# Decoding the last chunk of two token matrices in the mix stage instead of in attention

## The chip, the cores and the metric

The kernel runs on one core of a Trainium2 chip. The metric is device time in microseconds (us) of one execution. Engines by the names of the profile: PE is TensorE (matmuls; PEld its weight loads), DVE is VectorE, ACT is ScalarE, POOL is GpSimd, SP is SyncE, which here only issues transfers. Each engine takes its instructions strictly in the order in which they stand.

## What is computed

Block-sparse attention (4 batches, 8 heads, 768 positions, 64 features a head, blocks of 32) and then a token and channel mix on its output.

```python
mask = |blk_i - blk_j| <= 1, or first or last block row or column, or 3 sampled blocks per row
attn = softmax(where(mask, q @ k.T / 8, -1e9));  x = (attn @ v), heads side by side   # (4, 768, 512)
theta = x @ w_theta
zr, zi = x * cos(theta), x * sin(theta)
y = einsum('ts,bsd->btd', w_tok_r, zr) + einsum('ts,bsd->btd', w_tok_i, zi)
u = x + y
out = u + maximum(u @ w_ch, 0)
```

The four weight matrices arrive as 64-bit numbers and are turned into pairs of 32-bit numbers, a high and a low part, on the chip: the "decoding" of this text. Every matrix product of the mix is done three times, high by high, high by low and low by high.

## The kernel before

**Attention.** A work list of 52 units: per pair of batches four wide units (first and last block rows) and 22 ordinary ones, one block row each. The order of all engines is written out by hand in a loop over the units (`manual_schedule`). For a unit, POOL gathers keys and values, PE makes the scores (L308), DVE the negated maximum (L310), ACT the exponentials (L319), PE turns them (L325), ACT copies them out (L327), PE weighs the values (L359), and after every second unit DVE normalises (L340 to L344) and SP writes the rows to a buffer `xs` in DRAM.

**Decoding.** A `Piece` is a stretch of columns of one weight matrix on 128 partitions. Its work is in three phases: `bits` (L71 to L73 on DVE, after L67 on ACT), `rest` (L79, L81) and `low` (L90, L91, after the cast L87 on ACT, which is `high`). The `Decoder` goes through a list of pieces; `ahead(n)` puts the ACT instructions of the next n phases into the order and `go(n)` the DVE ones. Two pieces' raw words are loaded at first, and a piece's load (L62) is issued on SP when the piece two places before it has had its last phase. In attention the list holds `w_theta` (4 pieces of 512 columns) and both token matrices (9 each): 22 pieces, 66 phases, spread over the units by weight (no phases in the first and last two units).

A token matrix is six chunks of 128 rows by 768 columns. Chunks 0 and 1 have tiles of their own (`w_tok_r_hi`, ...). Chunks 2 to 5 go to a `room` that attention uses for keys or values at first, and that is taken over (`settle`) when the first piece for it is cast.

**The mix.** 48 steps, 12 a batch: step k has batch b, half h of the channels (6 steps each) and chunk j of the tokens. For a step PE makes the angles (`theta`, L654 to L656), ACT and DVE reduce them (`reduced`, L661 to L666), ACT takes sine and cosine, DVE multiplies by x (L681), ACT casts the high parts zh (L686) and DVE makes the low parts zl (L690), two steps before PE uses them in `mix` (24 matmuls, L706 to L708). For h = 0 DVE also turns rows (L637) and splits them (L646). SP loads x for a later step in eight transfers (L609, L622). After chunk 5 of a half DVE adds x (L719 to L722). A batch's eight output products (`out`, 12 matmuls, L729 to L731, into one bank, emptied by L734 and L735) wait in a list and are done two at a time in the second to fifth steps of the next batch, the last batch's at the end.

The first steps' preparation is woven into the last units of attention by hand. Steps 0 to 4 are also in the order written (`theta(k+2)`, `waves(k+1)`, `turn(k+3)`, `turned(k+1)`, `split(k+3)`, `reduced(k+2)`, loads, decoding, `mix(k)`); from step 5 on a scheduler, which simulates the engines, sets the order of each engine, and may draw an instruction of a later step into an earlier place. `w_ch` is decoded in the mix: 8 pieces of 256 columns, with `PHASES` (1, 1, 1, 3, 3) in steps 0 to 4 and 3 phases in each of steps 7 to 11.

Of the kernel before, what the change touches and what calls it, by code (L numbers as in the profile page):

```python
# [26 lines left out]
Q_BUFS = 3  # L27
XO_BUFS = 2
FIXED = 5
PHASES = (1, 1, 1, 3, 3)  # L30

# [551 lines left out]
def token_mix(tc, w, ch_pieces, xs, outT, bias, nb, fore):  # L585
# [7 lines left out]
    nc = tc.nc  # L593
    with ExitStack() as late, ExitStack() as ctx:
        half_pi, up_int, down_int, early = bias
# [3 lines left out]
        def at(k):  # L599
            return k // 12, (k // 6) % 2, k % 6  # L600
# [26 lines left out]
        def turn(k, tag="r"):  # L627
            b, h, j = at(k)
            if h:
                return  # L630
            if j % 3 == 0:
                tp = tps[min((2 * b + j // 3) % 3, 1)]
                xT[b, j // 3] = [tp.tile([P, 4, 384], F32R, tag=f"xT{x}", name=f"xT{x}{b}_{j}") for x in "hl"]
            raw = xr.pop((b, j))
            turning[k] = r = xp.tile([P, 4, 128], F32, tag=tag, name=f"r{k}", bufs=3 if tag == "xa" else 1)
            for c in range(4):
                nc.vector.transpose(r[:, c, :].rearrange("p (i t) -> p i t", t=32), raw[:, :, c])  # L637
# [10 lines left out]
        def theta(k):  # L648
            b, h, j = at(k)
            hi, lo = tok(b, j)  # L650
            wh, wl = [x[:, :, 256 * h : 256 * h + 256] for x in w["theta"]]
            angles[k] = ps = ps_h.tile([P, 512], F32, tag="h", name=f"h{k}")[:, 0:256]
            for c in range(4):
                nc.tensor.matmul(ps, hi[:, c, :], wh[:, c, :], start=c == 0, stop=False)  # L654
                nc.tensor.matmul(ps, hi[:, c, :], wl[:, c, :], start=False, stop=False)  # L655
                nc.tensor.matmul(ps, lo[:, c, :], wh[:, c, :], start=False, stop=c == 3)  # L656
# [11 lines left out]
        def waves(k):  # L668
            r = angles[k]
            cs = tz.tile([P, 256], F32, tag="cs", name=f"cs{k}")  # L670
            nc.scalar.activation(cs, r, AF.Abs)  # L671
            nc.scalar.activation(cs, cs, AF.Sin, bias=half_pi, scale=-1.0)
            nc.scalar.activation(r, r, AF.Sin)
            angles[k] = cs, r
# [17 lines left out]
        def turned(k):  # L692
            multiplied(k)
            highs(k)
            lows(k)
# [43 lines left out]
        place = vp.tile([P, 6, 260], F32, tag="vw", name="xr_first").rearrange("p c f -> p (c f)")  # L739
# [5 lines left out]
        decoder = Decoder(ch_pieces(), None, nc.sync, fore)  # L745
# [40 lines left out]
        for k in range(FIXED):  # L786
            theta(k + 2)
            waves(k + 1)
            turn(k + 3)
            turned(k + 1)  # L790
            split(k + 3)
            reduced(k + 2)
            load(k + 3)
            load_raw(k + 5)
            phases = PHASES[k] if k < len(PHASES) else 0
            decoder.ahead(phases)
            decoder.go(phases)
            mix(k)
# [4 lines left out]
        for k in range(FIXED, steps):  # L803
            b, h, j = at(k)
            if k + 4 < steps:
                load(k + 4)
            if k + 5 < steps:
                load_raw(k + 5)
            if k + 2 < steps:
                theta(k + 2)  # L810
                reduced(k + 2)
                waves(k + 2)
                turned(k + 2)
            if k + 3 < steps:
                turn(k + 3)
                split(k + 3)
            if k > 6 and decoder.left():
                decoder.ahead(3)
                decoder.go(3)
            mix(k)  # L820
            if h == 0 and b > 0 and 0 < j < 5:
                for _ in range(2):
                    out(*pending.pop(0), ps_o, "o")
            if h == 1 and j == 5:
                pending += [(b, th, e) for th in range(2) for e in range(4)]
# [4 lines left out]
def sparse_attention_then_token_mix(ctx, tc, qT, qE, kT, vr, sampled, w_theta, w_tok_r, w_tok_i, w_ch, outT):  # L830
    nc = tc.nc
    n_batch = outT.shape[0]
    const = ctx.enter_context(tc.tile_pool(name="const", bufs=1))
    ident = const.tile([P, P], F32, name="ident")
    make_identity(nc, ident)
    bias = []
    for name, value in (("half_pi", math.pi / 2), ("up_int", ROUND), ("down_int", -ROUND), ("early", 0.0)):
        bias.append(const.tile([P, 1], F32, name=name))
        nc.vector.memset(bias[-1], value)
    dram = ctx.enter_context(tc.tile_pool(name="dram", bufs=1, space=bass.MemoryType.DRAM))  # L840
    xs = [dram.tile([NB, 2, 32, 2, 2, P], F32, name=f"xs{bp}") for bp in range(NP)]

    w = {}
    w["theta"] = [const.tile([P, 4, 512], F32R, name=f"w_theta_{x}") for x in ("hi", "lo")]
    for name in ("tok_r", "tok_i"):
        w[name] = [const.tile([P, 2, 768], F32R, name=f"w_{name}_{x}") for x in ("hi", "lo")]

    def room(name, use, dtype=F32):
        return const.tile([P, 8, 768], dtype, tag=f"room_{name}", name=f"{use}_{name}")

    def settle(name):
        t = room(name, "w", F32R)
        w[name] = [x[:, j] for x in w[name] for j in range(2)]
        w[name] = [w[name][2 * x : 2 * x + 2] + [t[:, 4 * x + j] for j in range(4)] for x in range(2)]
        return [t[:, 4 * x : 4 * x + 4] for x in range(2)]

    words = {n: a.bitcast(I32) for n, a in dict(theta=w_theta, tok_r=w_tok_r, tok_i=w_tok_i, ch=w_ch).items()}

    def pieces(name, f, place, at=0, total=3072):
        if place:  # L860
            total = place[0].shape[1] * place[0].shape[2]
        made = []
        for f0 in range(0, total, f):
            made.append(Piece(nc, place, slice(f0, f0 + f), words[name][:, 2 * (at + f0) : 2 * (at + f0 + f)], f"{name}_{at + f0}"))
        return made


    fore = ctx.enter_context(tc.tile_pool(name="fore", bufs=2))
    follow = token_mix(tc, w, lambda: pieces("ch", 256, w["ch"], total=2048), xs, outT, bias, n_batch, fore)
    next(follow)  # L870
    early = pieces("theta", 512, w["theta"])
    early += [x for pair in zip(pieces("tok_r", 512, w["tok_r"]), pieces("tok_i", 512, w["tok_i"])) for x in pair]
    for name in ("tok_r", "tok_i"):
        place = []
        early += pieces(name, 512, place, 1536)
        early[-6].before = lambda name=name, place=place: place.extend(settle(name))
    attention(tc, qT, qE, kT, vr, sampled.bitcast(I32), xs, ident, early, room, follow)
    for _ in follow:
        pass
# [48 lines left out]
```

## Time and profile before

| | us |
|---|---|
| median of 3 runs (588.4 to 591.17) | 588.78 |
| the profiled execution | 592.62 |
| its span in the trace | 590.8 |
| first matmul of the mix, after the span's start | 252.9 |

The page gives the busy time of each engine, then the span in 40 slices of 14.77 us (a digit is the busy share in tenths). Matmuls overlap each other, so a busy PE is not PE at its peak. The chain of waits follows the work that ended last back to the start. In a group's row stand line, engine, operation, output and inputs, count, then busy us, mean ns of one, and the engine's idle time just before them with what ended it. A bracket in a timeline row is the idle time before that instruction and its releaser. A row of the table of stretches gives busy us and count of each engine that has work in it.

### The profile page before, as it was taken

Reading aid. Unit: us, or ns where it says so; the run is one execution under the profiler, and the core shown is the slowest. Engines: PE = TensorE matmul, PEld = TensorE weight load, DVE = VectorE, ACT = ScalarE, POOL = GpSimd, SP = SyncE. Lnnn points to the kernel's source line nnn. Section 1 sums busy time; section 2 is a strip of 40 time slices with the busy share of each in tenths; the row PEclk is TensorE's granted clock in tenths of the full one; section 3 lists DMA queues with packets and bytes.
Section 4 is the critical chain, followed back from the end, with each engine's and each line's share of the span. In section 5 each row is a group of like instructions: output and inputs, shape, how many; then the busy total and the mean of one; then the engine's idle time right before and its main releaser. Section 6 shows DMA issues by size and latency. Waiting matters only on the chain.

```text
span 590.8 us, 16785 instructions
## 1 busy us (share of the span) xinstructions
PE 538.4 (91%) x6636; PEld 475.3 (80%) x6636; DVE 442.8 (75%) x997; ACT 342.7 (58%) x730; POOL 148.6 (25%) x262
## 2 busy tenths in 40 slices
PE   4897878888977977999999999999999999999997
PEld 2564555656645645799999999999999999999996
DVE  3788788878897988888989976648857549547554
ACT  2677666868776876865657443456634547434510
POOL 1477758841775977000000000000000000000000
PEclk9999998999998989999999999999999999999999
DMA  8979999886698998644332341211432111212002
GB/s 293 340 223 344 308 332 348 287 267 223 185 299 257 304 307 225 193 121 131 108 85 76 96 130 59 72 45 54 130 92 70 50 53 42 80 56 75 2 1 107
DMA packets 63263, 95.60 MB, mean 162 GB/s; under 512 B 9168, under 2 KB 44624, under 8 KB 63184
## 3 DMA queue, kind: packets, MB, share of 16 engines
q1 hardware_dynamic: 56848, 71.09, 39.0%
q0 software_dynamic: 6336, 23.43, 12.2%
q8 instruction: 52, 0.85, 0.6%
q14 instruction: 27, 0.22, 0.1%
HBM read 81.90 MB, written 12.58 MB: 160 GB/s over the span
## 4 chain that ended last, share of the span: by engine, by line
PE 68%; DVE 15%; ACT 8%; issue 4%; DMA 4%; SPq 1%; ACTq 0%; DVEq 0%
PE y L706 11%; PE y L707 11%; PE y L708 11%; PE X L359 4%; PE o L730 4%; PE o L729 4%; PE o L731 4%; PE T L325 4%; DVE m L310 3%; PE h L655 3%; PE h L654 3%; PE h L656 3%; ACT P L319 3%; PE S L308 3%; PE SW L401 2%
## 5 line engine op out<-in xcount | busy, mean ns | idle before, releaser
L319 ACT ACTIVATE P<-S,m 128x256 f32<-128x256 f32 x176 | 69.5, 487 | 15.2 <-DVE m L310 15.2
L325 PE MATMUL T<-ident,P 128*128 128x128 f32 x352 | 50.9, 285 | 15.0 <-ACT pT L327 10.4
L310 DVE TENSOR_REDUCE m<-S 128x4 f32<-128x1024 f32 x44 | 53.6, 1217 | 12.3 <-PE S L308 12.3
L327 ACT COPY pT<-T 128x1024 f32<-128x1024 f32 x44 | 44.9, 1021 | 30.5 <-PE T L325 30.4
L325 PEld LDWEIGHTS T<-ident,P 128*128 128x128 f32 x352 | 38.8, 143 | 27.8 <-ACT pT L327 18.3
L291 POOL DMA_INDIRECT vb<-in_vr_dram,rows x44 | 46.3, 1052 | 48.8 <-PE X L359 43.3
L308 PE MATMUL S<-kg,q 64*32 64x256 f32 x1408 | 52.8, 394 | 5.9 <-issue 5.9
L661 ACT ACTIVATE t<-h,up_int 128x256 f32<-128x256 f32 x48 | 22.6, 474 | 59.7 <-PE h L656 56.0
L269 POOL COPY kg<-kb 128x256 f32 (+2 forms) x101 | 50.9, 544 | 15.8 <-PE S L308 15.8
L269 POOL COPY kg<-kb_tok_i 128x256 f32 (+2 forms) x101 | 49.4, 530 | 21.1 <-DMA kb_tok_i<-in_kT_dram 14.9
L654 PE MATMUL h<-w_theta_hi,xTh 128*128 128x256 f32 x192 | 54.1, 282 | 0.4 <-ACT xTh L645 0.4
L656 PE MATMUL h<-w_theta_hi,xTl 128*128 128x256 f32 x192 | 54.1, 282 | 0.2 <-DVE xTl L646 0.2
L655 PE MATMUL h<-w_theta_lo,xTh 128*128 128x256 f32 x192 | 53.9, 281 | 0.0
L706 PE MATMUL y<-w_tok_r,zh 128*128 128x384 f32 x128 | 43.1, 337 | 1.1 <-ACT zh L686 1.1
L706 PE MATMUL y<-w_tok_i,zh 128*128 128x384 f32 x128 | 43.1, 337 | 0.0
L707 PE MATMUL y<-w_tok_r,zh 128*128 128x384 f32 x128 | 43.1, 337 | 0.0
L707 PE MATMUL y<-w_tok_i,zh 128*128 128x384 f32 x128 | 43.1, 336 | 0.0
L708 PE MATMUL y<-w_tok_r,zl 128*128 128x384 f32 x128 | 43.0, 336 | 0.0
L730 PE MATMUL o<-ul,w_ch_hi 128*128 128x384 f32 x128 | 42.9, 335 | 0.0
L731 PE MATMUL o<-uh,w_ch_lo 128*128 128x384 f32 x128 | 42.9, 335 | 0.0
L729 PE MATMUL o<-uh,w_ch_hi 128*128 128x384 f32 x128 | 42.6, 336 | 0.1
L671 ACT ACTIVATE cs<-rr 128x256 f32<-128x256 f32 x48 | 19.7, 414 | 39.1 <-DVE rr L666 38.9
(155 smaller groups left out, 1427.4 us busy)
## 6 DMA issues: line engine op xcount, KB each, us to landing
xa<-xs SPq DMA_DIRECT2D x192, 64.0 KB
out_dram<-of SPq DMA_DIRECT2D x32, 192.0 KB
va<-in_vr_dram SPq DMA_DIRECT2D x22, 260.0 KB
q<-in_qT_dram SPq DMA_DIRECT2D x22, 256.0 KB
xs<-xo SPq DMA_DIRECT2D x88, 64.0 KB
xr<-xs SPq DMA_DIRECT2D x84, 64.0 KB
raw_tok_r<-in_w_tok_r_dram SPq DMA_DIRECT2D x9, 512.0 KB
raw_tok_i<-in_w_tok_i_dram SPq DMA_DIRECT2D x9, 512.0 KB
```

What stands on the lines that cost most here:

```text
L269: nc.gpsimd.tensor_copy(dst, blocks.rearrange("r g s f -> r s g f"))
L308: nc.tensor.matmul(sc[32 * p : 32 * p + 32, e, b, :], q[rows, b, p, :], keys[rows, :, :, place(b, p), :], start=True, stop=True)
L310: nc.vector.tensor_reduce(m, sc, axis=AX.X, op=ALU.min)
L319: nc.scalar.activation(pt[:, e, b, :], sc[:, e, b, :], AF.Exp, bias=m[:, e, b : b + 1], scale=-1.0)
L325: nc.tensor.transpose(t[:, k, :], pt, ident)
L654: nc.tensor.matmul(ps, hi[:, c, :], wh[:, c, :], start=c == 0, stop=False)
L655: nc.tensor.matmul(ps, hi[:, c, :], wl[:, c, :], start=False, stop=False)
L656: nc.tensor.matmul(ps, lo[:, c, :], wh[:, c, :], start=False, stop=c == 3)
L706: nc.tensor.matmul(acc, zh[:, dd], wh[j][:, tt], start=j == 0 and m == 0, stop=False)
L707: nc.tensor.matmul(acc, zh[:, dd], wl[j][:, tt], start=False, stop=False)
L708: nc.tensor.matmul(acc, zl[:, dd], wh[j][:, tt], start=False, stop=j == 5 and m == 1)
L730: nc.tensor.matmul(ps, wh[:, c, :], ul, start=False, stop=False)
```

## The change

Of the chunks 2 to 5 in the `room` of each token matrix, attention decodes the first 2304 of 3072 columns (chunks 2 to 4: four pieces of 512 and one of 256), so its list has 20 pieces and 60 phases. Chunk 5 of both, 768 columns each, is decoded in the mix by the decoder that decodes `w_ch`: six pieces of 256 columns ahead of the eight of `w_ch`. `PHASES` now covers steps 0 to 13: 18 phases in steps 0 to 4, which finish the six token pieces, 18 in steps 6 to 10 and 6 in steps 12 and 13, which are the eight pieces of `w_ch`. Mix step 5 is the first to need chunk 5. The output products of a batch go into the third, fourth and fifth step of the next batch, three, three and two; the second step has none. `w_ch` is complete with step 13, the second of batch 1. Line numbers above 30 grow by one.

```diff
-PHASES = (1, 1, 1, 3, 3)
+PHASES = (3, 3, 4, 4, 4, 0, 4, 4, 4, 3, 3, 0, 3, 3)
+LATER = 2304
@@ for k in range(FIXED): @@
-            phases = PHASES[k] if k < len(PHASES) else 0
+            phases = PHASES[k]
             decoder.ahead(phases)
             decoder.go(phases)
             mix(k)
@@ for k in range(FIXED, steps): @@
-            if k > 6 and decoder.left():
-                decoder.ahead(3)
-                decoder.go(3)
+            if k < len(PHASES):
+                decoder.ahead(PHASES[k])
+                decoder.go(PHASES[k])
             mix(k)
-            if h == 0 and b > 0 and 0 < j < 5:
-                for _ in range(2):
+            if h == 0 and b > 0:
+                for _ in range((0, 0, 3, 3, 2, 0)[j]):
                     out(*pending.pop(0), ps_o, "o")
@@ pieces @@
-    def pieces(name, f, place, at=0, total=3072):
-        if place:
-            total = place[0].shape[1] * place[0].shape[2]
+    def pieces(name, f, place, at=0, span=None):
         made = []
-        for f0 in range(0, total, f):
-            made.append(Piece(nc, place, slice(f0, f0 + f), words[name][:, 2 * (at + f0) : 2 * (at + f0 + f)], f"{name}_{at + f0}"))
+        first, last = span or (0, place[0].shape[1] * place[0].shape[2])
+        for f0 in range(first, last, f):
+            f1 = min(f0 + f, last)
+            made.append(Piece(nc, place, slice(f0, f1), words[name][:, 2 * (at + f0) : 2 * (at + f1)], f"{name}_{at + f0}"))
         return made
-    follow = token_mix(tc, w, lambda: pieces("ch", 256, w["ch"], total=2048), xs, outT, bias, n_batch, fore)
+    rests = dict(tok_r=[], tok_i=[])
+
+    def mix_pieces():
+        made = [x for n, place in rests.items() for x in pieces(n, 256, place, 1536, (LATER, 3072))]
+        return made + pieces("ch", 256, w["ch"], span=(0, 2048))
+
+    follow = token_mix(tc, w, mix_pieces, xs, outT, bias, n_batch, fore)
-    for name in ("tok_r", "tok_i"):
-        place = []
-        early += pieces(name, 512, place, 1536)
-        early[-6].before = lambda name=name, place=place: place.extend(settle(name))
+    for name, place in rests.items():
+        made = pieces(name, 512, place, 1536, (0, LATER))
+        made[0].before = lambda name=name, place=place: place.extend(settle(name))
+        early += made
```

## The prediction

> **What bounds the kernel now.** I read the page first: the busy line, the slices and the chain of waits.
>
> ```profile
> span 590.8 us, 16785 instructions
> PE 538.4 (91%) x6636; PEld 475.3 (80%) x6636; DVE 442.8 (75%) x997; ACT 342.7 (58%) x730; POOL 148.6 (25%) x262
> PE   4897878888977977999999999999999999999997
> DVE  3788788878897988888989976648857549547554
> DMA  8979999886698998644332341211432111212002
> PE 68%; DVE 15%; ACT 8%; issue 4%; DMA 4%; SPq 1%; ACTq 0%; DVEq 0%
> ```
>
> There are two stages. Up to about 252 us (slice 17, 14.77 us each) attention runs with nothing at nine tenths for long but the DMA engines. From slice 17 on TensorE is at nine tenths in every slice. The table of stretches then gives the room beside it (columns: stretch, length, busy us and count of PE, PEld, DVE, ACT, POOL, then granted clock, DMA share and GB/s).
>
> ```profile
> 28.00:125.00 97.00, 80.36 (x1940) 55.71 (x1938) 82.46 (x130) 71.50 (x142) 69.21 (x115) 0.98 0.93 298
> 147.00:244.00 97.00, 80.17 (x1936) 56.57 (x1935) 83.32 (x132) 71.27 (x143) 65.61 (x109) 0.96 0.87 260
> 257.00:285.00 28.00, 28.00 (x186) 28.00 (x185) 23.77 (x76) 17.71 (x44) 0.00 (x0) 1.00 0.47 134
> 285.00:324.00 39.00, 37.73 (x239) 37.20 (x238) 36.32 (x109) 25.16 (x68) 0.00 (x0) 1.00 0.29 81
> 371.00:400.00 29.00, 29.00 (x185) 29.00 (x185) 16.18 (x42) 15.01 (x36) 0.00 (x0) 1.00 0.16 49
> ```
>
> In attention VectorE (85%), TensorE (83%) and the DMA engines (93% and 87%) are all close to full, so no one of them is the bound by itself. In the mix TensorE has no gap in 257 to 285, while VectorE is 85% busy there and 93% in 285 to 324: whatever is given to VectorE here has little room. From 371 on VectorE is half idle. The one wait of TensorE of over 0.4 us inside the mix stands in the timeline, and its releaser is a chain of ScalarE behind VectorE:
>
> ```profile
> 303.29 0.45 PE L706 MATMUL y<-w_tok_r,zh 128*128 128x384 f32 x1 [1.12 <-ACT zh L686]
> ```
>
> **What leaves attention.** Decoding one piece is seven VectorE instructions (bits 3, rest 2, low 2) and two of ScalarE. The stretch table for the tile da alone counts six of the seven (the first two rows: 9 pieces each of tok_r and tok_i, 512 columns; the third: 8 pieces of w_ch, 256 columns); the seventh, L81, comes from the groups by shape.
>
> ```profile
> 0.00:591.00 591.00, 35.64 (x54) 11.74 (x18) 0.99 0.52 162
> 0.00:591.00 591.00, 35.50 (x54) 12.16 (x18) 0.99 0.52 162
> 0.00:591.00 591.00, 16.48 (x48) 6.54 (x16) 0.99 0.52 162
> L81 DVE SCALAR_TENSOR_TENSOR raw_tok_r<-raw_tok_r,ds_tok_r 128x512 f32<-128x512 uint32 x9 | 6.5, 718 | 0.3
> L81 DVE SCALAR_TENSOR_TENSOR raw_ch<-raw_ch,ds_ch 128x256 f32<-128x256 uint32 x8 | 3.4, 422 | 0.1
> ```
>
> A 512-column piece costs (35.64 + 35.50) / 18 + 0.72 = 4.67 us of VectorE and 1.33 us of ScalarE; a 256-column piece 16.48 / 8 + 0.42 = 2.48 us and 0.82 us. Attention now decodes 18 token pieces of 512 columns; changed, 14 of 512 and 2 of 256. VectorE loses 4 x 4.67 - 2 x 2.48 = 13.7 us there, and the queue three loads' worth, 3 x 512 KB = 1.6 MB. What of the 13.7 us was on the path? The chain inside attention, a piece of it where VectorE leads throughout, and the two long transfers on it:
>
> ```profile
> 185.96 1.22 DVE m L310
> 187.19 0.61 DVE da_tok_i L71
> ...
> 203.91 0.76 DVE da_tok_i L73
> 204.68 1.15 DVE m L310
> 383 pieces in order of time: start us, us, what
> 75.94 8.68 DMA raw_tok_r<-in_w_tok_r_dram
> 151.32 5.42 DMA q<-in_qT_dram
> ```
>
> From 186 to 206 every step of the chain is VectorE, about half of it decoding; 29 to 51, 106 to 123 and 156 to 167 read the same. Elsewhere the chain goes through TensorE and ScalarE, or the two transfers. Adding up the 383 pieces of the chain from 28 to 244 us, decoding is 38.6 of 217 us. The four theta pieces stay, so 13.7 of some 102 us of decoding (22 pieces of 4.67) goes, 13.4%: 5.2 us by the chain. By the DMA engines, if they bind: 1.6 MB at the 298 GB/s of 28 to 125 us, 5.3 us. If VectorE's sum alone set the pace, 13.7 us. Below, 2 us, if the TensorE and ScalarE loop takes over at once. I take **6.5 us** off, nearer to the chain than to the whole sum, since VectorE is 85% busy, not 100%. The units keep their weights, so each now has 60/48 = 1.25 phases instead of 66/48 = 1.375; no instruction of attention itself moves.
>
> **What enters the mix.** Six pieces of 256 columns, 6 x 2.48 = 14.9 us on VectorE and 4.9 us on ScalarE, and six loads of 256 KB on SP, all in steps 0 to 5; w_ch's eight pieces follow in steps 6 to 13 instead of 0 to 11. VectorE takes its instructions in the order in which they stand. In step 0 (rr is the reduced angle, da and w_ch the piece, r a turned row block), before:
>
> ```order
> L664 SCALAR_TENSOR_TENSOR rr_4658<-t_4655,h_4619 128x256
> L665 SCALAR_TENSOR_TENSOR rr_4658<-t_4655,rr_4658 128x256
> L666 TENSOR_SCALAR rr_4658<-rr_4658 128x256
> L71 TENSOR_SCALAR da_ch_4672<-da_ch_4672 128x256
> L72 TENSOR_SCALAR da_ch_4672<-da_ch_4672 128x256
> L73 SCALAR_TENSOR_TENSOR da_ch_4672<-raw_ch_4261,da_ch_4672 128x256
> L637 STREAM_TRANSPOSE r_4722<-xr_4_4352 128x128 x4
> ```
>
> and changed:
>
> ```order
> L667 TENSOR_SCALAR rr_4632<-rr_4632 128x256
> L72 TENSOR_SCALAR da_tok_r_4646<-da_tok_r_4646 128x256
> L73 TENSOR_SCALAR da_tok_r_4646<-da_tok_r_4646 128x256
> L74 SCALAR_TENSOR_TENSOR da_tok_r_4646<-raw_tok_r_4235,da_tok_r_4646 128x256
> L80 TENSOR_SCALAR ds_tok_r_4651<-da_tok_r_4646 128x256
> L82 SCALAR_TENSOR_TENSOR raw_tok_r_4235<-raw_tok_r_4235,ds_tok_r_4651 128x256
> L91 TENSOR_TENSOR da_tok_r_4646<-da_tok_r_4646,w_tok_r 128x256
> L92 TENSOR_TENSOR w_tok_r<-da_tok_r_4646,raw_tok_r_4235 128x256
> L638 STREAM_TRANSPOSE r_4704<-xr_4_4326 128x128 x4
> ```
>
> A whole piece now stands ahead of the next step's transposes, where three of its instructions stood. Counting such rows up to the last zl that a mix step needs: up to zl of step 4, 24 decode instructions instead of 7 and four more transposes (0.2 us each); step 5, 33 instead of 14; step 13, 79 instead of 56; step 15, 94 instead of 56 but four output instructions fewer. At 2.48 / 7 = 0.354 us each, VectorE comes 6.8, 6.7, 8.1 and 38 x 0.354 - 4 x 0.555 = 11.2 us later if nothing gives. How early it is now:
>
> ```profile
> 281.56 0.42 DVE L690 TENSOR_TENSOR zl<-rr,zh 128x256 fp32r<-128x256 f32 x1
> 282.27 0.34 PE L706 MATMUL y<-w_tok_r,zh 128*128 128x384 f32 x1
> 324.41 0.42 DVE L690 TENSOR_TENSOR zl<-rr,zh 128x256 fp32r<-128x256 f32 x1
> 325.41 0.34 PE L706 MATMUL y<-w_tok_r_hi,zh 128*128 128x384 f32 x1
> 258.56 0.34 PE L706 MATMUL y<-w_tok_r_hi,zh 128*128 128x384 f32 x1
> 264.16 0.33 PE L706 MATMUL y<-w_tok_r,zh 128*128 128x384 f32 x1
> 267.97 0.70 DVE L637 STREAM_TRANSPOSE r<-xr 128x128 f32<-128x128 f32 x3 [0.95 <-DMA xr<-xs]
> 309.11 0.29 DVE L71 TENSOR_SCALAR da_ch<-da_ch 128x256 f32<-128x256 f32 x1 [1.45 <-ACT da_ch L67]
> 320.14 0.43 DVE L681 TENSOR_TENSOR cs<-cs,xa 128x256 f32<-128x256 f32 x1 [0.96 <-ACT cs L672]
> L734 DVE TENSOR_TENSOR of<-uh,ul 128x384 f32<-128x384 f32 x32 | 17.7, 555 | 14.2 <-DMA out_dram<-of 14.1
> ```
>
> The first two pairs of rows are the last zl of a step and the first matmul of its mix, for steps 5 and 13; the next two are the first matmuls of steps 1 and 2, 24 mix and 12 angle matmuls apart: 5.6 us, 0.156 us a matmul. Step 5's zl is done at 281.98, its mix starts at 282.27 and uses zl eight matmuls later (1.2 us): a lead of 1.5 us. Step 13's lead is 0.6 us. The gaps noted in VectorE's timeline from 252.7 us on sum to 2.3 us by step 5 and 7.4 by step 13; the three rows with a bracket are the largest. I let 60% of them be used (some are round trips to ScalarE that stay). Step 5 is then 6.7 - 1.4 - 1.5 = 3.8 us late, less the 1.12 us wait that TensorE no longer meets at 303: 2.7. Step 13: 8.1 - 4.4 - 0.6 = 3.1. These are one lag, not two, so the larger counts. With all gaps used it is 1.8, with none 7.5. I add 0.4 us for loads that land late (below) and take **3.5 us**.
>
> The deferred matmuls of step 5 show that the sixth chunk is only just ready. On TensorE, changed (y_2 and y_3 are the token columns that need the chunk's later pieces):
>
> ```order
> L707 MATMUL y_0_5182<-w_tok_r_hi,zh_7_5069 128x384
> L708 MATMUL y_0_5182<-w_tok_r_lo,zh_7_5069 128x384
> ...
> L708 MATMUL y_2_4661<-w_tok_i,zh_5_4958 128x384
> L709 MATMUL y_2_4661<-w_tok_i,zl_5_4959 128x384
> L708 MATMUL y_3_4662<-w_tok_i,zh_5_4958 128x384
> L709 MATMUL y_3_4662<-w_tok_i,zl_5_4959 128x384
> ```
>
> Step 5 ends after step 7 has begun, with angle products between; before, it ended ahead of step 6. TensorE has other work while it waits, so this costs nothing by itself.
>
> The outputs' move (three, three and two in a batch's third to fifth steps) I cost at nothing: they are the same matmuls, and VectorE, which empties their one bank, is busy 16 of 29 us in 371 to 400. Without that cover it is one output's two instructions per batch, 3 x 1.1 = 3.3 us.
>
> Sum: -6.5 + 3.5 = -3.0 us. The profiled execution took 592.62 us (span 590.8), and becomes 589.6; the median of the runs shown lies 3.8 us below it, so 588.78 becomes **585.8 us**.
>
> **The rivals.** *VectorE sets attention's whole pace.* For it:
>
> ```profile
> L310 DVE TENSOR_REDUCE m<-S 128x4 f32<-128x1024 f32 x44 | 53.6, 1217 | 12.3 <-PE S L308 12.3
> L344 DVE TENSOR_TENSOR xo<-X,sm 128x512 f32<-128x512 f32 x22 | 15.2, 691 | 0.8
> L73 DVE SCALAR_TENSOR_TENSOR da_tok_r<-raw_tok_r,da_tok_r x9: 691/759/2011, 65.5 to 176.5; 128x512 int32<-128x512 int32 x9
> ```
>
> 22 units take 97 us in each half, about 4 us each without the two transfers above; VectorE's own sum per unit is a minimum of 1.2 us, half a normalisation (0.35 and two small ones) and 1.375 phases of 1.56 us, 3.8 us. Against it: the gaps. Most of the 13.7 us, say 11, comes off: -11 + 3.5, 581.3 us. [...]
>
> *Attention is bound by the rest.* DMA share 0.93, and the loop of TensorE and ScalarE that leads from 206 to 244: 2.5 us come off, the mix takes 3: 589.3 us.
>
> *The loads decide, and it is slower.* A piece's load is issued when the piece two before it is done, and its first instruction, on ScalarE, stands ahead of the zh casts that TensorE waits for.
>
> ```profile
> ACT da_ch L67 <- DMA raw_ch<-in_w_ch_dram: 8.1, 4, 3.4
> 297.71 2.69 DMA raw_ch<-in_w_ch_dram
> ```
>
> Now four such waits cost ScalarE 2.0 us each, with six loads in the mix; twelve will be there. If the six new ones each hold up a cast by 2.0 us, the mix pays 12 instead of 3.5: +5.5, 594.3 us. It decides where a piece follows its second predecessor in less than the 2.7 us of a load plus SP's queue; in steps 0 to 4 a step is 5.6 us, which speaks against it, in steps 6 to 8 four phases leave less. [...] The 1.12 us wait above left the clock at 1.00.
>
> **How the numbers follow.** About 0.5%, 2.9 us, is what a measurement here can tell from no change. Forecast 0.42 (its own range 582.5 to 588.5; half of it beyond 0.5%), VectorE-paced 0.22, rest-bound 0.16, loads 0.20. Faster: 0.22 + 0.22 + 0.02; slower: 0.20 + 0.04; the rest is no change. The range runs from just under the VectorE-paced case to the nearer half of the loads' case, 579.5 to 592.5 us.
>
> **What would show it.** Right: the first mix matmul (now 252.9 us) comes 5 to 8 us earlier, decoding in attention falls by about 14 us of VectorE, and TensorE waits 3 to 5 us in all between steps 2 and 15, behind VectorE or a zh cast. Wrong: a start that moves by under 3 us or over 10; waits of ScalarE for raw loads of over 15 us; TensorE waiting after step 17, which would mean that the outputs cost something.

## The result and the profile after

The changed kernel takes 586.39 us (median of 21 runs, 582.05 to 593.48); the kernel before, run beside it, 589.26 us (median of 21). The ratio is 0.9932, 95% interval 0.9909 to 0.9955: faster by 0.7%, 4.0 us; it leaves out each kernel's slow executions, while the medians, 2.9 us apart, include them. Two later measurements of the same kernel on other occasions gave 0.9918 and 0.9924. The profiled execution took 591.0 us, more than the median, so stretches are compared below, not totals.

The page of the changed kernel, with its busy line, slices and chain:

```profile
span 589.2 us, 16834 instructions
PE 542.5 (92%) x6636; PEld 479.7 (81%) x6636; DVE 439.8 (75%) x1025; ACT 343.6 (58%) x738; POOL 146.5 (25%) x262
PE   4897887788989889988899999999999999999997
DVE  2788688678887978798899997558858459556554
PE 71%; DVE 11%; ACT 8%; issue 5%; SPq 3%; DMA 2%; ACTq 0%; DVEq 0%
```

VectorE's share of the chain falls from 15% to 11%. Its busiest slices in the mix, counted from 0, are now 20 to 23 (295 to 353 us), where they were 21 and 22. The stages are told apart by the first and last matmul of the mix. The timeline of TensorE, the first two rows of the changed kernel, the last of the kernel before (its first is 252.90):

```profile
243.32 0.41 PE L707 MATMUL y<-w_tok_r_hi,zh 128*128 128x384 f32 x1 [0.34 <-DVE xo L345]
585.25 0.34 PE L732 MATMUL o<-uh,w_ch_lo 128*128 128x384 f32 x1
```
```profile
586.30 0.34 PE L731 MATMUL o<-uh,w_ch_lo 128*128 128x384 f32 x1
```

Attention ends 9.6 us earlier (252.90 to 243.32). The mix, first to last matmul, takes 341.9 us instead of 333.4: 8.5 us of the 9.6 are given back. The stretches of attention, changed (same columns as before):

```profile
28.00:125.00 97.00, 80.76 (x1954) 56.86 (x1952) 78.62 (x125) 70.96 (x140) 68.36 (x115) 0.98 0.94 299
147.00:244.00 97.00, 86.64 (x2076) 63.62 (x2061) 81.79 (x150) 77.39 (x156) 64.41 (x109) 0.98 0.88 259
```

VectorE is busy for 3.8 us less in the first stretch, yet TensorE gets through about the same number of matmuls (1954 for 1940). The gain appears in the second: 2076 for 1936. Where in it shows TensorE's timeline. The first three rows are of the kernel before, the others the same groups of matmuls in the changed kernel (the 27th and the 31st group of score matmuls, and between them the only waits of over a microsecond whose releaser reads "issue": nothing that the profile shows):

```profile
161.95 1.09 PE L308 MATMUL S<-kg,q 64*32 64x256 f32 x32
180.91 0.53 PE L359 MATMUL X<-vb,pT 128*32 128x65 f32 x5 [3.27 <-issue]
184.76 1.09 PE L308 MATMUL S<-kg,q 64*32 64x256 f32 x32
```
```profile
161.21 1.09 PE L309 MATMUL S<-kg,q 64*32 64x256 f32 x32
174.69 0.33 PE L360 MATMUL X<-vb,pT 128*32 128x65 f32 x5 [1.07 <-issue]
177.10 1.09 PE L309 MATMUL S<-kg,q 64*32 64x256 f32 x32
```

The lead grows from 0.74 to 7.66 us between the two groups, and ends only 1.9 us higher at the first mix matmul. The kernel before waits 3.27 us there, 2.2 us more, and its clock is halved (0.50 granted) from 180.8 to 184.2 us, which costs up to 1.7 us and has no counterpart in the changed kernel. The chain of waits that the prediction read has this wait among its five longest pieces; the prediction gave it no term.

In the mix, these are all the waits of TensorE, from its timeline; before there was one, of 1.12 us at 303.29:

```profile
254.59 0.39 PE L655 MATMUL h<-w_theta_hi,xTh 128*128 128x256 f32 x1 [1.28 <-ACT xTh L646]
255.31 0.40 PE L657 MATMUL h<-w_theta_hi,xTl 128*128 128x256 f32 x1 [0.23 <-DVE xTl L647]
271.35 0.44 PE L707 MATMUL y<-w_tok_r,zh 128*128 128x384 f32 x1 [0.48 <-ACT zh L687]
279.07 0.44 PE L707 MATMUL y<-w_tok_r,zh 128*128 128x384 f32 x1 [1.78 <-ACT zh L687]
287.30 0.41 PE L707 MATMUL y<-w_tok_r_hi,zh 128*128 128x384 f32 x1 [0.39 <-DVE uf L720]
291.20 0.44 PE L707 MATMUL y<-w_tok_r_hi,zh 128*128 128x384 f32 x1 [1.19 <-ACT zh L687]
```

The sum is 5.35 us, all within the first 48 us. Steps counted by the order of TensorE's matmuls, the rows at 271.35, 279.07 and 291.20 open the mix of steps 4, 5 and 7; the first two stand ahead of step 2. The second part of the loss is the granted clock (third column from the right), in the three-microsecond stretches behind two of these waits; it was 1.00 throughout this part before:

```profile
255.00:258.00 3.00, 2.77 (x13) 2.69 (x13) 2.61 (x8) 1.05 (x3) 0.00 (x0) 0.59 0.46 133
258.00:261.00 3.00, 3.00 (x16) 3.00 (x16) 2.80 (x11) 1.85 (x6) 0.00 (x0) 0.84 0.21 37
279.00:282.00 3.00, 2.93 (x10) 2.93 (x11) 2.17 (x7) 3.00 (x10) 0.00 (x0) 0.57 0.61 155
282.00:285.00 3.00, 3.00 (x22) 3.00 (x21) 2.68 (x10) 1.60 (x5) 0.00 (x0) 0.86 0.33 88
```

Each dip costs 3 x (0.41 + 0.16) or 3 x (0.43 + 0.14) = 1.7 us of full clock.

That VectorE is what runs late shows in equally long stretches, the changed kernel first, then the kernel before:

```profile
249.50:279.10 29.60, 25.84 (x155) 24.75 (x154) 26.89 (x86) 15.30 (x39) 0.00 (x0) 0.94 0.47 134
253.00:282.60 29.60, 29.60 (x194) 29.60 (x195) 25.32 (x79) 17.91 (x44) 0.00 (x0) 1.00 0.49 134
```

VectorE is busy for 26.89 us instead of 25.32, and its waits of over 0.15 us sum to 1.3 us (0.22, 0.65 and 0.46), while TensorE, which had no wait in the stretch before, waits 3.8 us.

### The profile page after: what moved, and what is told of

The parts are those of the page before. It is cut to its first block, busy times and chain, and to the rows that moved or that the text cites. A ratio compares the mean times of both kernels' runs of the same rounds, so it can differ in the third digit from the quotient of the medians.

```text
span 589.2 us, 16834 instructions
## 1 busy us (share of the span) xinstructions
PE 542.5 (92%) x6636; PEld 479.7 (81%) x6636; DVE 439.8 (75%) x1025; ACT 343.6 (58%) x738; POOL 146.5 (25%) x262
## 4 chain that ended last, share of the span: by engine, by line
PE 71%; DVE 11%; ACT 8%; issue 5%; SPq 3%; DMA 2%; ACTq 0%; DVEq 0%
PE y L707 10%; PE y L709 10%; PE y L708 10%; PE X L360 6%; PE T L326 5%; PE o L732 4%; PE o L730 4%; PE o L731 4%; PE h L656 3%; PE h L657 3%; PE h L655 3%; PE S L309 3%; ACT P L320 3%; ACT pT L328 3%; DVE m L311 2%
## 5 line engine op out<-in xcount | busy, mean ns | idle before, releaser
L309 PE MATMUL S<-kg,q 64*32 64x256 f32 x1408 | 51.5, 382 | 5.6 <-issue 5.5
L292 POOL DMA_INDIRECT vb<-in_vr_dram,rows x44 | 44.7, 1016 | 41.7 <-PE X L360 36.1
L707 PE MATMUL y<-w_tok_r,zh 128*128 128x384 f32 x128 | 44.1, 344 | 2.3 <-ACT zh L687 2.3
L708 PE MATMUL y<-w_tok_r,zh 128*128 128x384 f32 x128 | 44.0, 343 | 0.0
```

Source lines behind the costliest of these rows:

```text
L309: nc.tensor.matmul(sc[32 * p : 32 * p + 32, e, b, :], q[rows, b, p, :], keys[rows, :, :, place(b, p), :], start=True, stop=True)
L707: nc.tensor.matmul(acc, zh[:, dd], wh[j][:, tt], start=j == 0 and m == 0, stop=False)
L708: nc.tensor.matmul(acc, zh[:, dd], wl[j][:, tt], start=False, stop=False)
```

## The experiments

**Theory after the first look (A).** Attention gains about 9 us; the mix pays because VectorE has more to do in steps 0 to 5 than TensorE, and each dip of the clock behind a wait adds 1.7 us. **Rivals.** It is not VectorE's sum but the place of the decoding in its order (B); it is loads and stores in the way of ScalarE; the mix is longer because it starts earlier on transfers of attention that have not landed.

One table for all runs; ratios are to the kernel before beside the same runs, the other columns from the profiled execution of each. "Dips" are the separate 1.7 us losses of the clock inside the mix.

| kernel | ratio (95%) | first mix matmul | mix | waits | dips |
|---|---|---|---|---|---|
| before | 1 | 252.90 | 333.4 | 1.12 | 0 |
| changed | 0.9932 (0.9909 to 0.9955) | 243.32 | 341.9 | 5.35 | 2 |
| changed, e5 | 0.9918 (0.9881 to 0.9955) | 242.45 | 340.6 | 5.11 | 1 |
| changed, e9 | 0.9924 (0.9892 to 0.9955) | 241.30 | 340.7 | 5.01 | 1 |
| e4 outputs only | 1.0055 (1.0022 to 1.0087) | 256.38 | 333.7 | 1.14 | 0 |
| e8 no sixth chunk, old pace | 0.9853 (0.9809 to 0.9897) | 242.48 | 334.3 | 1.47 | 0 |
| e1 no sixth chunk, new pace | 0.9979 (0.9948 to 1.0010) | 245.30 | 345.4 | 7.98 | 3 |
| e11 two thirds | 0.9923 (0.9886 to 0.9960) | 245.10 | 337.4 | 2.86 | 0 |
| e12 even pace | 0.9925 (0.9891 to 0.9958) | 240.69 | 341.6 | 4.42 | 2 |
| e10 decoding before the angle | 1.0091 (1.0056 to 1.0126) | 242.09 | 348.9 | 11.67 | 2 |
| e7 low parts on GpSimd | 1.0008 (0.9974 to 1.0043) | 239.11 | 344.2 | 7.62 | 0 |
| e6 load behind store | 0.9926 (0.9891 to 0.9962) | 239.64 | 340.9 | 5.30 | 1 |
| e2 transfers back | 0.9948 (0.9912 to 0.9985) | 246.24 | 338.3 | 4.34 | 0 |
| e3 VectorE work back | 1.0005 (0.9974 to 1.0035) | 242.15 | 341.0 | 5.23 | 1 |

Take the waits and 1.7 us for each dip from the length of the mix, and 332.3 to 334.5 us are left in every row but one (e7: 336.6). So what a variant pays in the mix is its waits and its dips. Eight rows have the very same attention (changed three times, e6, e7, e8, e10, e12), and their first mix matmul lies between 239.1 and 243.3: a single profile tells that instant to some 2 us. Part of this is the clock, with one to three dips ahead of it in these profiles.

### Outputs alone (e4)

The kernel before, with only the outputs moved:

```diff
-            if h == 0 and b > 0 and 0 < j < 5:
-                for _ in range(2):
+            if h == 0 and b > 0:
+                for _ in range((0, 0, 3, 3, 2, 0)[j]):
```

> The kernel before with the outputs' move alone: three, three and two products in a batch's third, fourth and fifth step. Theory (they cost nothing, other work hides them): ratio to before 0.998 to 1.002. Rival (three in one step wait for their one bank): three batches times 1 to 3 us, 1.005 to 1.015, with TensorE waits behind the bank's emptying.

The mix takes 333.7 us with one wait of 1.14 us, as before (333.4, 1.12): inside the mix the move costs nothing. The whole is 0.55% slower all the same; the profile shows the extra time in attention (first mix matmul 3.5 us later, 1.7 us of it a dip of the clock from 246.4 us), although attention's order is that of the kernel before. The ratio thus lies in the rival's range, but the rival's sign, waits behind the bank's emptying, is absent. Why attention is longer is not settled. It means that a ratio can differ here by half a per cent for a reason that the profiles do not name, and differences of that size below carry this reserve.

### The sixth chunk left out (e1, e8)

In both, the sixth chunk is neither loaded nor decoded in the mix; its columns are zeroed by GpSimd, so that part of the result is left out. They differ in the pace of `w_ch`, e1 first, e8 second:

```diff
-        made = [x for n, place in rests.items() for x in pieces(n, 256, place, 1536, (LATER, 3072))]
-        return made + pieces("ch", 256, w["ch"], span=(0, 2048))
+        return pieces("ch", 256, w["ch"], span=(0, 2048))
-PHASES = (3, 3, 4, 4, 4, 0, 4, 4, 4, 3, 3, 0, 3, 3)
+PHASES = (0, 0, 0, 0, 0, 0, 4, 4, 4, 3, 3, 0, 3, 3)
+PHASES = (1, 1, 1, 3, 3, 0, 0, 3, 3, 3, 3, 3, 0, 0)
```

> The changed kernel without the decode of chunk 5: GpSimd sets the chunk to zero at the start of the mix (so the output is not the reference's), and steps 0 to 4 decode nothing; w_ch stays in steps 6 to 13. This is attention's gain alone. Theory (attention gains about 9.6 us, the mix gives some 7 back in waits of TensorE and a lower clock behind them): the first mix matmul at about 243 us as in the changed kernel, TensorE waits under 2 us in all after it, and the time is 6 to 9 us below the changed kernel, 577 to 581 us. Rival (the profiled 9.6 us is one execution's luck, the true gain is some 4 us and the mix pays little): first mix matmul at 246 to 250 us, time 583 to 586 us.

e1 missed by far: less work, and a mix of 345.4 us. With steps 0 to 5 empty, the scheduler drew `w_ch`'s decoding forward, two pieces at a time, into places where their words had not landed. Waits of ScalarE and of VectorE in e1, 240 to 340 us:

```profile
ACT da_ch L68 <- DMA raw_ch<-in_w_ch_dram: 7.4, 3, 3.2
DVE da_ch L72 <- ACT da_ch L68: 7.9, 4, 3.3
```

So e1 isolates nothing, but it shows that the loads' rival is a real mechanism: three raw loads, 7.4 us in all, hold up ScalarE and with it VectorE. e8 repeats it with the old pace, which keeps `w_ch` where the kernel before had it.

> The changed kernel without the sixth chunk's decoding and loads (its columns are zeroed by GpSimd at the start of the mix, so the output is not the reference's), and with w_ch decoded at the pace that it had in the kernel before. What is left of the change is what attention gains. Theory: the first mix matmul stands where the changed kernel has it, 242 to 247 us, and the mix takes 333 to 335 us as before, with 1 to 2 us of waits and no dip of the clock: 0.983 to 0.989 of the kernel before, 5 to 8 us faster than the changed kernel. Rival (the mix is longer because it starts earlier, on transfers and results of attention that are not there yet, whatever is decoded in it): the mix takes over 338 us here too, and the time is that of the changed kernel within 2 us.

It came as theory A said. The mix is 334.3 us with 1.47 us of waits and no dip, though it starts 10.4 us earlier than in the kernel before; an early start by itself costs nothing. What is left is attention's gain: 1 - 0.9853 of 590.75 us is 8.7 us, with 0.9 us of a longer mix 9.6, which is also what the first pair of profiles shows (e8's own profile, 10.4). e5, the changed kernel in the same batch, stands at 0.9918: the sixth chunk in the mix costs 0.65%, 3.8 us, by the ratios; by the medians (587.08 and 581.95) 5.1 and by the two profiles' mixes 6.3. The first lies below the 5 to 8 us that were expected.

### How much of it (e11) and at what pace (e12)

> The changed kernel once more, beside the next three. Expected 0.990 to 0.996 of the kernel before, the mix 340 to 342 us from its first matmul to the last.

```diff
-PHASES = (3, 3, 4, 4, 4, 0, 4, 4, 4, 3, 3, 0, 3, 3)
-LATER = 2304
+PHASES = (2, 2, 2, 3, 3, 0, 4, 4, 4, 3, 3, 0, 3, 3)
+LATER = 2560
```

> Two thirds of the change: of the sixth chunk's three pieces per matrix only the last two are decoded in the mix (2, 2, 2, 3, 3, 0 phases in steps 0 to 5 instead of 3, 3, 4, 4, 4, 0), the first stays in attention. Theory A (VectorE's sum against TensorE's in steps 0 to 5 sets what the mix pays; 6 x 0.83 = 5.0 us less of it): the first mix matmul at 244 to 248 us, the mix 334 to 337 us with no dip of the clock, 0.985 to 0.991 of the kernel before, 1 to 3 us faster than the whole change. Rival (each part gains and pays in proportion): the mix 338 to 339 us, a time between the kernel before and the changed one.

The mix falls to 337.4 us and keeps its clock, but the start moves to 245.1: 0.9923, the same as the whole change. The expected gain of 1 to 3 us over the whole change did not come, and neither did the rival's time between the two kernels. None, two thirds and all of the chunk in the mix give 334.3, 337.4 and 340.6 to 341.9 us. By proportion two thirds would be 338.5 to 339.4; 337.4 lies between the theory's 337 and the rival's 338 and decides for neither. One reason why it is not shorter stands in its timeline of TensorE: the chunk is finished just too late for step 5, and TensorE waits for the cast of its last piece.

```profile
283.83 0.61 PE L707 MATMUL y<-w_tok_i,zh 128*128 128x384 f32 x2 [1.39 <-ACT w_tok_i L88]
```

Now the whole change with the decoding spread evenly:

```diff
-PHASES = (3, 3, 4, 4, 4, 0, 4, 4, 4, 3, 3, 0, 3, 3)
+PHASES = (3, 3, 3, 3, 3, 3, 3, 3, 3, 3, 3, 3, 3, 3)
```

> The changed kernel with three phases of decoding in every one of the steps 0 to 13 instead of 3, 3, 4, 4, 4, 0, 4, 4, 4, 3, 3, 0, 3, 3: the same 42 phases, the sixth chunk done one step later. Theory A (VectorE's sum): up to step 4 it has three phases, 2.5 us, less; the wait of 1.78 us shrinks below 1 us and its dip of the clock goes, but step 5 now waits for the chunk's last pieces by up to 1 us: the mix 338 to 341 us. Theory B (the place of the decoding between reduction and product decides): seven instructions instead of nine stand there, the wait is 0.7 us shorter, without a dip: the mix 338 to 339 us. If the chunk's last piece is what TensorE waits for, a wait behind w_tok_i or VectorE's last operation of a piece will stand in the list, and the mix takes over 341 us.

```profile
274.00 0.44 PE L707 MATMUL y<-w_tok_r,zh 128*128 128x384 f32 x1 [0.62 <-ACT zh L687]
281.72 0.44 PE L708 MATMUL y<-w_tok_i,zh 128*128 128x384 f32 x1 [1.10 <-DVE w_tok_i L92]
283.73 0.58 PE L655 MATMUL h<-w_theta_hi,xTh 128*128 128x256 f32 x1 [0.75 <-DVE rr L665]
```

The wait ahead of step 5 shrinks from 1.78 to 0.62 us, and the chunk's last piece takes its place (1.10 us, behind VectorE's L92): the mix stays at 341.6 us and the time at 0.9925, the third case of the expectation. A double dip begins at 282.2 us, behind that wait. Less before step 5 means a later chunk in step 5; the lag moves along the order.

### The order of the decoding (e10)

VectorE's timeline of the changed kernel ahead of the 1.78 us wait:

```profile
274.71 0.29 DVE L667 TENSOR_SCALAR rr<-rr 128x256 f32<-128x256 f32 x1
274.92 0.29 DVE L80 TENSOR_SCALAR ds_tok_i<-da_tok_i 128x256 int32<-128x256 int32 x1
...
277.82 0.43 DVE L82 SCALAR_TENSOR_TENSOR raw_tok_i<-raw_tok_i,ds_tok_i 128x256 f32<-128x256 uint32 x1
278.17 0.42 DVE L682 TENSOR_TENSOR cs<-cs,xa 128x256 f32<-128x256 f32 x1
```

and ScalarE's sine and cast there:

```profile
275.90 0.40 ACT L674 ACTIVATE rr<-rr 128x256 f32<-128x256 f32 x1
278.62 0.40 ACT L687 CAST zh<-cs 128x256 fp32r<-128x256 f32 x1 [2.31 <-DVE cs L682]
```

Nine decode instructions, 274.92 to 278.25, stand between the reduced angle and its product with x. The sine is done at 276.30, and the product could have begun then: 1.9 us earlier than 278.17, the length of the wait. Theory B takes this place to be the cause. e10 writes the same instructions ahead of the reduction:

```diff
+            decoder.ahead(phases)
+            decoder.go(phases)
             reduced(k + 2)
             load(k + 3)
             load_raw(k + 5)
             phases = PHASES[k]
-            decoder.ahead(phases)
-            decoder.go(phases)
             mix(k)
```

(the line with `phases` moves up with them)

> The changed kernel with the decoding of steps 0 to 4 written ahead of the reduction of the next angle instead of behind it: the same instructions, but no decoding stands any more between the reduction and the product with x, where TensorE's 1.78 us wait arises; in its place VectorE waits there for ScalarE's round trip, 1.3 to 1.9 us in each of five steps. Theory A (VectorE's sum decides: in steps 0 to 4 it has 26 us of its own and 15 us of decoding, against TensorE's 34 us): the wait does not go, it moves or grows, because VectorE's order does not change its sum and the round trips now lie open; the mix takes 341 to 345 us. Theory B (the place of the decoding decides): the 1.78 us wait and the dip of the clock behind it go, and the mix takes 337 to 339 us.

B falls in this form: the mix is 348.9 us, waits 11.67, two dips; 0.9% slower than the kernel before. It is worse than A had priced it (341 to 345). TensorE's waits in e10, by releaser:

```profile
PE y L707 <- ACT zh L687: 4.1, 2, 3.1
PE h L655 <- ACT xTh L646: 2.9, 2, 2.0
PE y L708 <- DVE w_tok_i L92: 2.1, 1, 2.1
```

Decoding behind the reduction covers ScalarE's round trip (275.00, the end of L667, to 276.30: 1.3 us here); ahead of it that time lies open, and everything comes later, the chunk's last piece too. The order of the changed kernel is the better one. So both count: the amount (e8, e11 and e12 have less of it ahead of step 5, and a shorter wait for zh there or none), and with the same amount the order, by 6.3 us of waits. VectorE's sum alone does not set the price.

### GpSimd for the low parts (e7)

```diff
-        self.nc.vector.tensor_tensor(self.a, self.a, self.hi.bitcast(F32), op=ALU.subtract)
-        self.nc.vector.tensor_tensor(self.lo, self.a, self.raw[:, :, 0].bitcast(F32), op=ALU.add)
+        engine = self.nc.vector if self.f == 512 or self.early else self.nc.gpsimd
+        engine.tensor_tensor(self.a, self.a, self.hi.bitcast(F32), op=ALU.subtract)
+        engine.tensor_tensor(self.lo, self.a, self.raw[:, :, 0].bitcast(F32), op=ALU.add)
```

(`early` is set for attention's two short pieces, which stay on VectorE)

> The changed kernel, with the last two operations of each of the mix's 14 pieces on GpSimd instead of VectorE: 28 operations, 9.9 us, leave VectorE in steps 0 to 13. Theory (VectorE's work is what delays zh in steps 4 to 8): the waits of 1.78 us near 279 us and 1.19 us near 291 us go, with the clock's dip behind the first, and the mix is 3 to 5 us shorter (337 to 339 us). [...] Rival (ScalarE's waits for raw loads decide): the waits stay where they are, the mix gains less than 1 us.

Slower than the changed kernel by 0.9% (1.0008 to 0.9918 in the same batch), and the mix is not 3 to 5 us shorter but 3.6 longer (344.2 to 340.6). The dip goes, but the wait ahead of step 5 shrinks only to 1.55 us, and new waits come later; VectorE's products with x take over 0.5 us. The groups by shape, 240 to 330 us, the first row of e5 and the second of e7, and e7's timeline of both engines around one GpSimd instruction:

```profile
L682 DVE TENSOR_TENSOR cs<-cs,xa 128x256 f32<-128x256 f32 x14 | 5.7, 406 | 0.0
```
```profile
L683 DVE TENSOR_TENSOR cs<-cs,xa 128x256 f32<-128x256 f32 x13 | 8.1, 621 | 0.0
289.52 4.93 POOL L92 TENSOR_TENSOR da_ch<-da_ch,w_ch_hi 128x256 f32<-128x256 f32 x1 [7.73 <-DVE da_ch L73]
294.53 0.79 POOL L93 TENSOR_TENSOR w_ch_lo<-da_ch,raw_ch 128x256 fp32r<-128x256 f32 x1
293.45 0.41 DVE L692 TENSOR_TENSOR zl<-cs,zh 128x256 fp32r<-128x256 f32 x1
293.79 0.94 DVE L683 TENSOR_TENSOR cs<-cs,xa 128x256 f32<-128x256 f32 x1
295.37 0.44 PE L733 MATMUL o<-uh,w_ch_lo 128*128 128x384 f32 x1 [1.40 <-POOL w_ch_lo L93]
```

VectorE's product with x grows from 406 to 621 ns, and one GpSimd subtraction takes 4.93 us where the other 13 take 0.95 on the mean (GpSimd's groups, 240 to 360 us), while VectorE runs without a gap beside it; TensorE then waits 1.40 us for that piece. The product's row above, in the last 0.7 us of the 4.93, takes 0.94 us, against 0.41 on the mean of e5; no VectorE instruction beside the 4.93 us takes over 0.54 us before that. Why GpSimd's subtraction took so long, and VectorE's product over twice its time, is not shown.

### The store at the change of stages (e6)

The 1.28 us wait at 254.59 goes back to a wait of ScalarE's first decode instruction for attention's last store (the bracket, in ScalarE's timeline of the changed kernel):

```profile
249.00 0.43 ACT L68 ACTIVATE da_tok_r<-raw_tok_r 128x256 f32<-128x256 f32 x1 [2.45 <-DMA xs<-xo]
```

e6 moves one load, four issues of SP, behind that store and nothing else:

```diff
             multiplied(0)
             split(2)
             highs(0)
-            load(2)
             yield
             lows(0)
             yield
+            load(2)
```

> The changed kernel itself, beside the next three on one chip, as their measure. Expected 0.991 to 0.996 of the kernel before; the first mix matmul at 242 to 247 us, 341 to 342 us from there to the last matmul, waits of TensorE inside the mix of 5 to 5.5 us, and a granted clock under 0.9 in the three microseconds behind the waits of 1.28 and 1.78 us.

> The changed kernel, with one issue of SP moved: the load of xa for mix step 2 (four transfers) now follows attention's last store of xs instead of preceding it. Nothing else changes on any engine. Theory (the first wait of the mix is that store's: ScalarE's first instruction of a piece needs the store's buffer): ScalarE's 2.45 us wait at the stage change shrinks by the 1.9 us of the four issues, TensorE's 1.28 us wait goes below 0.4 us, the clock stays at 1.00 there, and the mix is 1.0 to 3 us shorter (339 to 341 us). Rival (the wait is DVE's or a raw load's, the store only ends last): TensorE waits at the same place for something else, the mix stays at 341 to 342 us.

ScalarE's wait for the store is gone in e6; it is 1.13 us in e5, 1.61 in e9 and 2.45 in the first profile. TensorE's wait behind it is 0.21 us in e6, without a dip. But in the unchanged e5 it was 0.22 us, without a dip too: what could be had is 0 to 1.3 us of wait and a dip, depending on the execution. The mix (340.9 and 340.6 us) and the ratio (0.9926 and 0.9918) are the same; e5's mix lies just under the 341 to 342 that were expected of it. That the store holds ScalarE up is shown; what it costs TensorE is small in e5.

### What attention gained from (e2, e3)

e2 puts the bytes back: three transfers of 512 KB within DRAM, behind three of attention's raw loads. e3 puts VectorE's work back: behind each of 18 pieces one dead instruction like L74, 13 us in all.

```diff
+        if self.extra:
+            queue.dma_start(self.extra[0], self.extra[1])
```

```diff
+        if self.f == 512:
+            nc.vector.scalar_tensor_tensor(s.bitcast(F32), s.bitcast(F32), 1.0, self.a, op0=ALU.mult, op1=ALU.add)
```

> The changed kernel with the 1.6 MB put back on the DMA queue in attention: three transfers of 512 KB from DRAM to DRAM, behind the raw loads of the 7th, 12th and 17th piece; VectorE has nothing more to do. Theory (VectorE's work sets attention): first mix matmul within 2 us of the changed kernel's 243 us, time within 2 us of it. Rival (the DMA engines set attention): first mix matmul 5 us later, at about 248 us, and the time 4 to 5 us above the changed kernel.

> The changed kernel with 13 us put back on VectorE in attention: behind each of the 18 pieces of 512 columns one more instruction of that size (0.72 us, its result is never read), no transfer more. Theory (VectorE's work sets attention): first mix matmul 8 to 10 us later than the changed kernel's 243 us, at 251 to 253 us, time 8 to 10 us above the changed kernel. Rival (the DMA engines, or the loop of TensorE and ScalarE): first mix matmul at 244 to 247 us, time at most 4 us above.

By ratio, against 0.9925 (the mean of the three of the changed kernel), e2 gives back 0.23%, 1.4 us, inside its interval, and e3 0.80%, 4.7 us. By the ratios, then, VectorE's work weighs more than the bytes. But neither forecast fits e3: 4.7 us lies just above the rival's 4 and far below the theory's 8 to 10. The changed kernel was not run beside e2 and e3, and e4 of their batch shows 0.55% that nothing explains. Nor do the profiles separate them: e2's first mix matmul, at 246.24, lies between its two forecasts, and e3's, at 242.15, where the changed kernel has it (e3's profile was the quickest of its ten executions, 588.83 against a median of 591.52).

Both together are 6.1 of some 9.6 us by the ratios. What neither puts back is the place at 162 to 185 us. e4, whose attention is that of the kernel before, has the same wait, 3.27 us at 182.1, and a dip there; the changed kernel's other two profiles have 1.35 us (e5) and none (e9) and no dip; e2 and e3 have no dip there either, and their lead grows over the same groups by 6.8 and 7.0 us. So up to 4 us of attention's gain, 2.2 of the wait and 1.7 of the dip, come from a wait whose cause is not shown, and how VectorE's work or the loads could bring it about stays open.

## Why the prediction was right, and where its terms were not

The forecast was 585.8 us, -3.0; the median is 586.39, and the ratios of the three measurements say -4.0 to -4.8. The sign holds, and so does the outline: decoding leaves attention, which gains, and makes TensorE wait in the mix, which pays. Both terms of the sum were too small by 3 to 5 us, and that the sum came out all the same is luck: their errors cancel.

- **Attention, 6.5 us taken: 9.6 found** (the first pair of profiles, and e8; e5 and e9 start the mix 10.4 and 11.6 us before the kernel before's one profile). Decoding left, and somewhat more of it than worked out: the da instructions of the two token matrices in attention fall from 71.1 us to the sum of these two rows, 56.7 us, 14.5 less (columns: stretch, length, VectorE busy and count, clock, DMA share, GB/s; tok_r, then tok_i):

```profile
0.00:243.00 243.00, 27.91 (x48) 0.99 0.89 281
0.00:243.00 243.00, 28.75 (x48) 0.99 0.89 281
```

  That is six of the seven instructions; 4 x 35.57 / 9 - 2 x 2.06 = 11.7 us less was worked out for them. The pieces that stayed were quicker as well: 3.75 us for these six instead of 3.95, with 2.06 for each short one.

  The step that failed is "I take 6.5 us off, nearer to the chain than to the whole sum". The chain's share (5.2 us) counts only the places where decoding happened to be last, and puts nothing on the chain's wait of 3.27 us for nothing shown and the dip behind it, where the two kernels part. The rival that let VectorE set the whole pace (11 us) priced this term better than the forecast did, but e3 bears its mechanism out by half at most.
- **The mix, 3.5 us taken: 7.2 to 8.5 found.** The lag at step 5 was about right: 6.7 - 1.4 - 1.5 = 3.8 us late; the four waits up to step 5 sum to 1.28 + 0.23 + 0.48 + 1.78 = 3.77. So close a match is luck: 1.51 us of it goes back to the store, which had no term, and the same sum is 3.48 us in e5 and 3.43 in e9. That VectorE runs late is borne out by its stretch above, and that it is one lag too: after 291 us nothing waits. That TensorE by then runs late enough itself is the likely reason, not a tested one. Two steps failed. "Less the 1.12 us wait that TensorE no longer meets at 303": a wait of the same size and releaser, 1.19 us, stands ahead of step 7, and 0.39 ahead of step 6. So the waits are 4.2 us more than before instead of 2.7 to 3.1. And the clock had no term: of it stood only, under the loads' rival, "The 1.12 us wait above left the clock at 1.00". One or two dips of 1.7 us are the largest piece that was missing. Some 0.9 to 1.7 us more is not in the list of waits; the first matmul behind a wait takes 0.44 us instead of 0.34, which is part of it.
- **Loads, 0.4 us.** ScalarE's waits for raw words are 7.1 us (6 times) where they were 8.1 (4 times); none of those in the mix is for a token piece. The rival that these decide fell for this order; e1 shows an order in which they do.
- **Outputs, nothing.** Held inside the mix: no wait behind 291 us, and e4's mix is as long as before. e4's ratio of 1.0055 is not explained.
- **The rest-bound rival** (2.5 us off attention) fell with the first mix matmul.

Of the signs named ahead, the start came 9.6 us earlier in the first pair, between "right" (5 to 8) and "wrong" (over 10), and 10.4 and 11.6 us earlier in e5 and e9, which by that sign is wrong: attention's term was undersized. TensorE's waits from step 2 on are 3.84 us (4.89 in e5, 4.35 in e9), inside the 3 to 5 named as right; the clock, which had no term, stood under no sign.

## What to carry to other kernels

Moving work from one stage to another trades two rates. Here two thirds of the move paid as much as all of it, and an even pace as much as an uneven one; only leaving the work out paid more (0.985). Before filling the gaps of an engine that feeds TensorE, add up its work for each step against TensorE's: here some 15 us more on VectorE in steps 0 to 5 raised TensorE's waits in the mix from 1.12 us to between 5.0 and 5.4, and the same work in another order to 11.67. A wait ahead of a dense run of matmuls can cost more than its length: here 1.78 us cost 1.7 us of clock again, while 1.77 us in e2 did not. And read every long piece of the chain of waits, also one that waits for nothing shown: here up to 4 us of the gain stood behind one.

## What the runs showed of the hardware

- **The clock falls in portions.** Every dip in the mix lasted 3.41 us at half clock (0.50 granted), 1.7 us lost, or twice that in a row (by the clock of stretches of 0.2 us). Within one execution their starts lie whole multiples of 3.41 us apart: 255.55 and 279.44 us in the changed kernel (7), 273.83 and 294.31 in e10 (6), 267.29 and 284.36 in e1 (5). Waits of 1.28 and 0.23 us (the changed kernel), of 1.76 (e3), or of 0.38 and 1.10 us (e12), were followed by a dip.
- **The length of a wait alone does not tell whether one comes.** Waits of 1.76 to 1.78 us at step 5 were followed by a dip in e3, e5, e6, e9 and the changed kernel, and a wait of 1.77 us by none in e2. In e10 waits of 2.05 and 2.09 us (up to 254.2 and 285.9 us) had none, while 1.07 and 1.04 us, both between 270.4 and 273.4 us, had one. In the 3.41 us ahead of the start of a dip TensorE's waits come to 1.48 us in e12, 1.51 and 1.78 in the changed kernel, 1.76 to 1.78 in e3, e5, e6 and e9, 2.40 and 1.95 in e1, 2.11 and 2.8 in e10. What else decides is not shown.
- **GpSimd beside a full VectorE** took five times as long once (4.93 us against 0.95 on the mean of the other 13 subtractions, e7), and a VectorE product in the last 0.7 us of it over twice as long (0.94 us against 0.41 on the mean of e5).
